# Attention and MLP on one core: softmax sums and weighted values in four 32-column tiles of the PE array, 112-token key tiles, one load per pair and tensor

## The chip, the core and the metric

The kernel runs on one core of a Trainium2 chip. The core's engines run side by side, each through a program of its own in order, and wait for one another through semaphores: TensorE (PE; PEld is its loading of the stationary operand), VectorE (DVE), ScalarE (ACT), GpSimd (POOL) and SyncE (SP, which here only issues DMAs). Sixteen DMA engines move data between HBM and the on-chip memory. The metric is the time of one execution in microseconds (us), the median of the runs. [...]

## What is computed

The sizes are B = 8 batches, H = 12 heads, S = 448 tokens and D = 64 per head; the MLP is 768 to 2048 to 768.

```
scores = scale * np.matmul(q, k.transpose(0, 1, 3, 2))
m = np.max(scores, axis=-1, keepdims=True)
e = np.exp(scores - m)
attn = e / (np.sum(e, axis=-1, keepdims=True) + np.exp(-m) + 1e-09)
attn_out = np.matmul(attn, v)

x = attn_out.transpose(0, 2, 1, 3).reshape(B * S, H * D)
h = x @ w_in
sp = np.where(h > 20.0, h, np.log1p(np.exp(np.minimum(h, 20.0))))
out = (h * np.tanh(sp)) @ w_out
```

With the maximum cancelled, a weight is exp(s) / (1 + sum of exp(s)). The kernel computes it so: no maximum is taken, and the reciprocal is exp(-ln(1 + sum)).

## The kernel before

The unit of attention is a **pair** j: two heads of one batch, 48 pairs in all, six to a batch. The program goes slot by slot. Slot j holds the scores of pair j, the weighted values of pair j-1, the loads of pair j+4 and the casts of pair j+2, and between them pieces of MLP work, called units: `mm1` is one block of 128 hidden columns of the batch before (six matmuls of 448 columns), `mm2` half of one block of the output of the batch before that (eight matmuls of 384 columns). Batch p = 0 (slots 0 to 5) has no units, batch p = 1 (slots 6 to 11) only mm1 units, later batches both. The order on every engine is the order of this text, since the schedule is manual.

Scores are computed transposed: keys on the partitions, queries along the columns. The 448 keys of a head are three tiles of 128 and a tail of 64. Each full tile of the two heads is two matmuls (L165), each of 64 rows, one in the upper and one in the lower half of the array. The tails of both heads stand in one 128-row block-diagonal tile `k_tail` and take one matmul (L177). ACT writes the exponentials `e` (L172 for full tiles, L178 for the tail).

`attend` multiplies `e` with `v_aug`, whose 128 columns are the 64 values of one head beside 64 columns of ones, so that one result `av` holds the weighted values in one half of its partitions and the sum of the weights, repeated, in the other half. It takes six matmuls of 128 rows (L188) and two of 64 rows for the tails (L197). ACT makes ln(1 + sum) of each head (L205) and exp(-ln) of both (L206), and `normalize` multiplies on DVE, one head at a time (L216), into `xT`, the transposed input of the MLP.

Loads of a pair are seven DMAs on SP: the first 384 tokens of q, k and v for both heads (L79: qm, km, vm), the tails of q and k (L91) and two tails of v (L86). POOL casts to bfloat16 (L104, L107, L113, L114). For pairs of batch 0 PE transposes q and k (L141, L146) and DVE copies the result; for the others two DMA transposes on SP do it (L121 for the full tiles, L125 for the tails), after which POOL copies the tail of k into `k_tail` (L137).

PSUM has three pools of two buffers: `s_ps` for scores (two banks each), `x_ps` for `av` and PE transposes, `m_ps` for mm1 and mm2 results. After the last mm1 unit of a batch (slot i = 4 of the next) `mish` runs on ACT over all of `h_sb` (L249, L250) between two loads of ACT's function table; mm2 reads its result `gm`. While it runs PE has eight mm2 units of the older batch, in p = 1 none. The weights are loaded by POOL's queue, `w_in` in slots 1 to 4 and `w_out` in slots 6 to 9. Slot 48 attends the last pair, and the MLP of the last batch ends the program.

Of the kernel before, what the change touches and what calls it, by code (L numbers as in the profile page):

```python
# [8 lines left out]
FP32 = mybir.dt.float32  # L9
# [6 lines left out]
def kernel(  # L16
# [11 lines left out]

    nc = tc.nc
# [36 lines left out]
    for i in range(2):
        kt = singles.tile([128, 128], BF16, name=f"k_tail{i}")
        nc.vector.memset(kt, 0.0)
        k_tail.append(kt)

    loaded, cast, qk_t, e_t, av_t, x_t = {}, {}, {}, {}, {}, {}
    gm_t, gt_t = {}, {}

    def load(j):
        b, h0 = j // NPAIR, 2 * (j % NPAIR)
        tiles = {}
        for name, src in (("q", q), ("k", k), ("v", v)):
            main = stage.tile([128, 2, NT, D], FP32, tag=f"{name}m", name=f"{name}m")
            nc.sync.dma_start(  # L79
                out=main,  # L80
                in_=src[b, h0 : h0 + 2, 0:MAIN, :].rearrange("h (p t) d -> p h t d", t=NT),
            )
            if name == "v":
                tail = stage.tile([128, D], FP32, tag="vt", name="vt")
                for h in range(2):
                    nc.sync.dma_start(  # L86
                        out=tail[h * 64 : h * 64 + 64, :], in_=src[b, h0 + h, MAIN:S, :]
                    )
            else:
                tail = stage.tile([64, 2, D], FP32, tag=f"{name}t", name=f"{name}t")  # L90
                nc.sync.dma_start(  # L91
                    out=tail, in_=src[b, h0 : h0 + 2, MAIN:S, :].rearrange("h p d -> p h d")
                )
            tiles[name] = (main, tail)
        loaded[j] = tiles

    def do_cast(j):

        tiles = loaded.pop(j)
        mb = half.tile([128, 2 * NT, 2, D], BF16, tag="mb", name="mb")  # L100
        tb = half.tile([64, 2, 2, D], BF16, tag="tb", name="tb")
        for i, name in enumerate(("k", "q")):
            main, tail = tiles[name]
            nc.gpsimd.tensor_copy(  # L104
                out=mb[:, i * NT : (i + 1) * NT].rearrange("p t h d -> p h t d"), in_=main
            )
            nc.gpsimd.tensor_copy(out=tb[:, 1 - i], in_=tail)  # L107
        main, tail = tiles["v"]
        va = v_aug[j % NV]
        vr = va[:, 0 : 2 * NT, :].rearrange("p (t h) c -> p t h c", h=2)  # L110
        for h in range(2):
            c = h * D
            nc.gpsimd.tensor_copy(out=vr[:, :, h, c : c + D], in_=main[:, h, :, :])  # L113
            nc.gpsimd.tensor_copy(  # L114
                out=va[h * 64 : h * 64 + 64, 2 * NT, c : c + D],
                in_=tail[h * 64 : h * 64 + 64, :],
            )
        cast[j] = (mb, tb)
        if j >= NPAIR:
            qk = qk_pool.tile([128, 2 * S], BF16, tag="qk", name="qk")  # L120
            nc.sync.dma_start_transpose(  # L121
                out=qk[:, 0 : 2 * MAIN].rearrange("p (t c) -> p t c", c=128),
                in_=mb.rearrange("p t h d -> p (t h d)"),
            )
            nc.sync.dma_start_transpose(  # L125
                out=qk[:, 2 * MAIN : 2 * S].rearrange("p (t c) -> p t c", c=TAIL),
                in_=tb.rearrange("p t h d -> p (t h d)"),
            )
            qk_t[j] = qk

    def transposes(j):
        mb, tb = cast.pop(j)
        kt = k_tail[j % 2]
        if j >= NPAIR:
            for h in range(2):
                r = slice(h * 64, h * 64 + 64)
                nc.gpsimd.tensor_copy(out=kt[r, r], in_=qk_t[j][r, S + MAIN : 2 * S])  # L137
            return
        ps = x_pool.tile([128, 1024], BF16, tag="x", name="tr_ps")
        for t in range(2 * NT):  # L140
            nc.tensor.transpose(  # L141
                ps[:, t * 128 : (t + 1) * 128], mb[:, t].rearrange("p h d -> p (h d)"), ident
            )
# [269 lines left out]
```

## Time and profile before

| | us |
|---|---|
| median of 3 runs | 492.85 |
| lowest and highest | 492.05, 496.56 |
| the profiled execution | 497.37 |
| its span, first to last instruction | 495.6 |
| PE busy in the span | 441.5 |
| ACT busy | 297.9 |
| DVE busy | 169.6 |
| POOL busy | 144.6 |

The profiled execution is 4.5 us above the median of the runs. Its time is its span and 1.8 us around it. Busy time of PE contains the time in which a matmul passes through the array behind the next one, so what one matmul costs is read from the distance between starts. [...]

### The profile page before, as it was taken

The page shows a single profiled execution, that of the slowest core. Times are in us where ns is not written, and L with a number is a line of the kernel's source. Part 1 is how long each engine was busy: PE and PEld are TensorE (multiplying, and loading weights), DVE is VectorE, ACT ScalarE, POOL GpSimd, SP SyncE. Part 2 cuts the span into 40 slices and gives each one's busy share as a digit, 9 for nine tenths or more (in the row PEclk, how much of TensorE's full clock was granted, in tenths as well). Part 3 has the DMA queues.
Part 4 walks back from the last instruction along what each step waited for, and adds up shares of the span by engine and source line. Part 5 has one row for each costly group of instructions (what it writes and reads, how often), then busy time and mean ns, then how long its engine had stood idle before and what let it go on. Part 6 is the DMA issues. An engine that isn't in the chain of part 4 may idle for free.

```text
span 495.6 us, 7105 instructions
## 1 busy us (share of the span) xinstructions
PE 441.5 (89%) x2432; PEld 209.9 (42%) x2432; DVE 169.6 (34%) x288; ACT 297.9 (60%) x419; POOL 144.6 (29%) x482
## 2 busy tenths in 40 slices
PE   3677595828999899999998999999998999999995
PEld 1222142304445344554444444554453445555563
DVE  4222242402463155322651354325532444220121
ACT  3556553595669667765678675856776757643200
POOL 4544253423333144313342243232431430000000
PEclk9956697977999999999999999999999999999999
DMA  5699999951543464446453564365544620120112
GB/s 132 157 219 238 163 211 158 199 131 20 159 113 90 119 164 117 117 134 170 119 132 103 129 160 118 92 165 148 131 110 121 162 57 1 63 65 1 60 69 64
DMA packets 110373, 60.46 MB, mean 122 GB/s; under 512 B 64768, under 2 KB 106752, under 8 KB 110336
## 3 DMA queue, kind: packets, MB, share of 16 engines
q1 hardware_dynamic: 105088, 53.71, 42.8%
q0 software_dynamic: 5248, 6.29, 8.2%
q8 instruction: 19, 0.31, 0.3%
q14 instruction: 18, 0.15, 0.1%
HBM read 45.61 MB, written 11.01 MB: 114 GB/s over the span
## 4 chain that ended last, share of the span: by engine, by line
PE 80%; DMA 7%; ACT 6%; SPq 3%; POOL 1%; issue 1%; DVE 0%; POOLq 0%
PE o_ps L264 30%; PE h_ps L221 29%; PE av_ps L188 10%; PE s_ps L165 6%; DMA qk<-tb 3%; PE av_ps L197 3%; PE s_ps L177 2%; DMA vm<-in_v_dram 2%; ACT e L172 1%; ACT ln L205 1%; ACT gm L249 1%; DMA km<-in_k_dram 1%; DMA vt<-in_v_dram 1%; SPq L79 1%; ACT rc L206 1%
## 5 line engine op out<-in xcount | busy, mean ns | idle before, releaser
L221 PE MATMUL h_ps<-xT,w_in_sb 128*128 128x448 bf16 x768 | 158.6, 356 | 1.4 <-DVE xT L216 1.4
L172 ACT ACTIVATE e<-s_ps 128x896 bf16<-128x896 f32 x144 | 126.0, 909 | 32.8 <-PE s_ps L165 30.5
L264 PE MATMUL o_ps<-w_out_sb,gm 128*128 128x384 bf16 x768 | 132.0, 330 | 0.0
L205 ACT ACTIVATE ln<-av_ps 64x448 f32<-64x448 f32 x96 | 51.7, 539 | 117.8 <-PE av_ps L197 116.6
L229 DVE COPY h_sb<-h_ps 128x448 f32<-128x448 f32 x112 | 70.0, 625 | 108.2 <-PE h_ps L221 107.4
L221 PEld LDWEIGHTS <-w_in_sb 128*128 128x128 bf16 x768 | 73.4, 99 | 72.3 <-issue 11.2
L264 PEld LDWEIGHTS <-gm 128*128 128x128 bf16 x768 | 75.4, 99 | 52.7 <-issue 4.3
L216 DVE TENSOR_TENSOR xT<-av_ps,rc 64x448 bf16<-64x448 f32 x96 | 59.7, 622 | 81.4 <-ACT rc L206 79.5
L165 PE MATMUL s_ps<-qk 64*128 64x448 bf16 x288 | 52.4, 384 | 37.0 <-ACT e L172 26.6
L272 DVE COPY o_sb<-o_ps 128x384 f32<-128x384 f32 x56 | 31.2, 558 | 116.9 <-PE o_ps L264 116.3
L137 POOL COPY k_tail_97<-qk 64x64 bf16<-64x64 bf16 x42 | 9.8, 234 | 112.9 <-DMA qk<-tb 72.3
L165 PEld LDWEIGHTS <-qk 64*128 64x128 bf16 x288 | 14.2, 96 | 61.2 <-issue 49.6
L249 ACT ACTIVATE gm<-h_sb 128x1536 bf16<-128x1536 f32 x28 | 39.2, 1471 | 0.1
L137 POOL COPY k_tail_95<-qk 64x64 bf16<-64x64 bf16 x42 | 9.8, 234 | 76.3 <-DMA qk<-tb 48.2
L104 POOL CAST mb<-km 128x384 bf16<-128x384 f32 x48 | 24.2, 503 | 19.8 <-DMA km<-in_k_dram 17.2
L206 ACT ACTIVATE rc<-ln 128x448 f32<-128x448 f32 x48 | 27.7, 576 | 1.5
L178 ACT ACTIVATE e<-s_ps 128x448 bf16<-128x448 f32 x48 | 25.7, 536 | 0.0
L104 POOL CAST mb<-qm 128x384 bf16<-128x384 f32 x48 | 24.2, 503 | 0.0
L264 PE MATMUL o_ps<-w_out_sb,gt 128*128 128x384 bf16 x128 | 22.0, 326 | 0.0
L233 ACT ACTIVATE gm<-h_ps 128x384 bf16<-128x384 f32 x16 | 7.9, 491 | 19.2 <-PE h_ps L221 19.2
L188 PE MATMUL av_ps<-e,v_aug_89 128*128 128x448 bf16 x72 | 18.0, 389 | 0.5 <-DVE k_tail_97 L153 0.5
L188 PE MATMUL av_ps<-e,v_aug_87 128*128 128x448 bf16 x72 | 18.0, 389 | 0.5 <-DVE k_tail_95 L153 0.5
(56 smaller groups left out, 262.7 us busy)
## 6 DMA issues: line engine op xcount, KB each, us to landing
qm<-in_q_dram SPq DMA_DIRECT2D x48, 192.0 KB, 2.8
km<-in_k_dram SPq DMA_DIRECT2D x48, 192.0 KB, 2.8
vm<-in_v_dram SPq DMA_DIRECT2D x48, 192.0 KB, 2.8
out_dram<-o_sb SPq DMA_DIRECT2D x24, 384.0 KB, 2.7
w_in_sb<-in_moe_w_in_dram POOLq DMA_DIRECT2D x4, 768.0 KB, 9.0
w_out_sb<-in_moe_w_out_dram POOLq DMA_DIRECT2D x4, 768.0 KB, 7.7
qt<-in_q_dram SPq DMA_DIRECT2D x48, 32.0 KB, 2.7
kt<-in_k_dram SPq DMA_DIRECT2D x48, 32.0 KB, 2.8
```

What stands on the lines that cost most here:

```text
L104: nc.gpsimd.tensor_copy(out=mb[:, i * NT : (i + 1) * NT].rearrange("p t h d -> p h t d"), in_=main)
L165: nc.tensor.matmul(sp[:, h, 0:S], lhsT=qk[r, t * 128 : (t + 1) * 128], rhs=qk[r, MAIN : MAIN + S], start=True, stop=True,)
L172: nc.scalar.activation(out=e[:, 2 * t : 2 * t + 2, :], in_=sp[:, :, 0:S], func=AF.Exp, scale=SCALE)
L188: nc.tensor.matmul(av[h][:, 0:S], lhsT=va[:, 2 * t + h, :], rhs=e[:, 2 * t + h, :], start=(t == 0), stop=False,)
L205: nc.scalar.activation(out=ln[r, :], in_=av[h][o, 0:S], func=AF.Ln, bias=1.0)
L206: nc.scalar.activation(out=rc, in_=ln, func=AF.Exp, scale=-1.0)
L216: nc.vector.tensor_mul(x_t[b][r, hp, :], av[h][r, 0:S], rc[r, :])
L221: nc.tensor.matmul(hp[:, 0:S], lhsT=w_in_sb[:, dm, ff * 128 : (ff + 1) * 128], rhs=x_t[b][:, dm, :], start=(dm == 0), stop=(dm == DM_T - 1),)
L229: nc.vector.tensor_copy(out=h_sb[:, ff, :], in_=hp[:, 0:S])
L249: nc.scalar.activation(out=gm[:, f, :], in_=h_sb[:, f, 0:MAIN], func=AF.Mish)
L264: nc.tensor.matmul(op[:, 0:HALF], lhsT=lhs, rhs=w_out_sb[:, ff, n * HALF : (n + 1) * HALF], start=(ff == 0), stop=(ff == FF_T - 1),)
L272: nc.vector.tensor_copy(out=o_sb[:, n * HALF : (n + 1) * HALF], in_=op[:, 0:HALF])
```

## The change

Attention goes by **groups** g of two pairs (four heads, three groups to a batch). The 448 keys are four tiles of 112 (token 4p + t on partition p of tile t), so there is no tail, no `k_tail` and no `v_aug`. Scores take eight matmuls per pair, two per tile, and four exponentials of 112 x 896. `sums(g)` adds up the weights of four heads: for each key tile four matmuls whose stationary operand is 112 x 32 ones and whose results go to partitions 0, 32, 64 and 96 on; ACT makes the reciprocal `rc` of all four heads with one Ln and one Exp. `attend(g, s)` does the same with 32 of the 64 value columns (every second one, s = 0 or 1), and one DVE multiplication writes `xT`. Both stand in even slots only, for the two pairs before. The rows of `w_in` are loaded in the order that fits. `den` and the PE transposes take buffers of `m_ps`.

Loads of a pair are three DMAs, in the order k, q, v, of 1,024 bytes per partition and head; they are issued after the casts and the DMA transpose of their slot, no longer ahead of them, and their staging has three buffers instead of four. One DMA transpose does q and k. DVE casts q and k of the pairs of batch 0, POOL the rest. `w_in` is loaded in slots 0 to 3 and `w_out` in slots 5 to 8. A block of 128 output rows is stored by two DMAs instead of one.

```diff
-    NT = S // 128
+    NT = 4
+    P = S // NT
-    stage = ctx.enter_context(tc.tile_pool(name="stage", bufs=4))
+    stage = ctx.enter_context(tc.tile_pool(name="stage", bufs=AHEAD - 1))
+    v_pool = ctx.enter_context(tc.tile_pool(name="v", bufs=6))
+    e_pool = ctx.enter_context(tc.tile_pool(name="e", bufs=3))
...
+        for name in names:
+            src = {"q": q, "k": k, "v": v}[name]
+            st = stage.tile([P, 2, NT * D], FP32, tag=name, name=f"{name}_f")
             nc.sync.dma_start(
+                out=st, in_=src[b, h0 : h0 + 2].rearrange("h (p t) d -> p h (t d)", t=NT)
+            )
...
+            nc.sync.dma_start_transpose(
+                out=qk.rearrange("c i (t p) -> c (i t) p", p=P),
+                in_=mb.rearrange("p i t h d -> p (i t h d)"),
+            )
...
+        ps = m_pool.tile([128, 2, S], BF16, tag="m", name="tr_ps")
...
+        for t in (2 * part, 2 * part + 1):
             sp = s_pool.tile([128, 2, 512], FP32, tag="s", name="s_ps")
             for h in range(2):
                 r = slice(h * D, h * D + D)
                 nc.tensor.matmul(
+                    sp[0:P, h, 0:S],
+                    lhsT=qk[r, 0, t * P : (t + 1) * P],
+                    rhs=qk[r, 1, :],
...
+    def side_by_side(ps, g, weights):
         for t in range(NT):
+            for c in range(4):
                 nc.tensor.matmul(
+                    ps[c * 32 : c * 32 + 32, 0:S],
+                    lhsT=weights(2 * g + c // 2, c % 2, t),
+                    rhs=e_t[2 * g + c // 2][:, t, c % 2, :],
                     start=(t == 0),
+                    stop=(t == NT - 1),
                 )
+    def sums(g):
+        den = m_pool.tile([128, 512], FP32, tag="m", name="den_ps")
+        side_by_side(den, g, lambda j, h, t: ones[0:P, :])
         rc = work.tile([128, S], FP32, tag="rc", name="rc")
+        nc.scalar.activation(out=rc, in_=den[:, 0:S], func=AF.Ln, bias=1.0)
+        nc.scalar.activation(out=rc, in_=rc, func=AF.Exp, scale=-1.0)
+        rc_t[g] = rc
+    def attend(g, s):
...
+        av = x_pool.tile([128, 512], FP32, tag="x", name="av_ps")
+        side_by_side(
+            av, g, lambda j, h, t: v_t[j][:, h, t, :].rearrange("p (d s) -> p s d", s=2)[:, s, :]
+        )
+        nc.vector.tensor_mul(x_t[b][:, gi, s, :], av[:, 0:S], rc_t[g])
...
-            if j + 4 < J:
-                load(j + 4)
+            g = j // 2 - 1 if j % 2 == 0 and j >= 2 else None
             if j + 2 < J:
-                do_cast(j + 2)
-            if 1 <= j <= 4:
-                load_w_in(j - 1)
-            if 6 <= j <= 9:
-                load_w_out(j - 6)
+                do_cast(j + 2, nc.vector if j + 2 < NPAIR else nc.gpsimd)
+                cast_v(j + 2)
+            if j + AHEAD < J:
+                load(j + AHEAD)
+            if j <= 3:
+                load_w_in(j)
+            if 5 <= j <= 8:
+                load_w_out(j - 5)
             rest = max(0, len(units) - 2)
             if j < J:
                 scores(j, 0)
             take(1)
             if j + 1 < J:
                 transposes(j + 1)
+            if g is not None:
+                sums(g)
             take(1)
-            if j >= 1:
-                attend(j - 1)
             if j < J:
                 scores(j, 1)
             take((rest + 1) // 2)
-            if j >= 1:
-                normalize(j - 1)
+            if g is not None:
+                attend(g, 0)
+                attend(g, 1)
             take(len(units), last=True)
```

On PE, before, the end of the weighted values of one pair (two results, av0 and av1, one per head) and the second half of the next pair's scores, then an mm1 unit:

```order
L188 LDWEIGHTS v_aug0_87
L188 MATMUL av1_ps_2047<-e_1926,v_aug0_87 128x448
L197 LDWEIGHTS v_aug0_87
L197 MATMUL av0_ps_2046<-e_1926,v_aug0_87 128x448
L197 LDWEIGHTS v_aug0_87
L197 MATMUL av1_ps_2047<-e_1926,v_aug0_87 128x448
L165 LDWEIGHTS qk_1829
L165 MATMUL s_ps_2061<-qk_1829 128x448
```

On PE, with the change, the end of an mm1 unit in an even slot and the first of four key tiles of a group's weighted values (`e` and `v_b` of its two pairs):

```order
L179 MATMUL h_ps_2475<-xT_1842,w_in_sb_88 128x448
L146 LDWEIGHTS v_b_1954
L146 MATMUL av_ps_2484<-e_2235,v_b_1954 32x448
L146 LDWEIGHTS v_b_1954
L146 MATMUL av_ps_2484<-e_2235,v_b_1954 32x448
L146 LDWEIGHTS v_b_2158
L146 MATMUL av_ps_2484<-e_2360,v_b_2158 32x448
L146 LDWEIGHTS v_b_2158
L146 MATMUL av_ps_2484<-e_2360,v_b_2158 32x448
```

Eight matmuls per pair with 128 result partitions became 24 with 32, of which four stand together, and they moved out of every slot into every second one.

On SP, before, one slot of a later batch, from two stores to the DMA transposes:

```order
L276 DMA out_dram<-o_sb 128x768 x2
L79 DMA qm<-in_q_dram 128x2x192
L91 DMA qt<-in_q_dram 64x2x64
L79 DMA km<-in_k_dram 128x2x192
L91 DMA kt<-in_k_dram 64x2x64
L79 DMA vm<-in_v_dram 128x2x192
L86 DMA vt<-in_v_dram 64x64 x2
L121 DMA_TRANSPOSE qk<-mb 128x6x128
L125 DMA_TRANSPOSE qk<-tb 128x2x64
```

On SP, with the change, such a slot:

```order
L219 DMA out_dram<-o_sb 112x768
L219 DMA out_dram<-o_sb 16x768
L92 DMA_TRANSPOSE qk<-mb 128x8x112
L77 DMA k_f<-in_k_dram 112x2x256
L77 DMA q_f<-in_q_dram 112x2x256
L77 DMA v_f<-in_v_dram 112x2x256
```

Nine issues for a pair became four, and the transpose moved ahead of the loads.

On ACT, before, around the `mish` of batch 1:

```order
L178 ACTIVATE e<-s_ps 128x448
L249 ACT_TABLE_LOAD
L249 ACTIVATE gm<-h_sb 128x1536 x4
L250 ACTIVATE gt<-h_sb 128x16x64
L251 ACT_TABLE_LOAD
L172 ACTIVATE e<-s_ps 128x896 x2
L205 ACTIVATE ln<-av_ps 64x448 x2
L206 ACTIVATE rc<-ln 128x448
L172 ACTIVATE e<-s_ps 128x896
```

On ACT, with the change, the same place:

```order
L159 ACTIVATE rc<-rc 128x448
L136 ACTIVATE e<-s_ps 112x896 x2
L207 ACT_TABLE_LOAD
L207 ACTIVATE gm<-h_sb 128x1536 x4
L208 ACTIVATE gt<-h_sb 128x16x64
L209 ACT_TABLE_LOAD
L136 ACTIVATE e<-s_ps 112x896 x6
L158 ACTIVATE rc<-den_ps 128x448
```

Behind `mish` six exponentials now stand in a row, where two Ln and an Exp stood after the first two.

## Rows read from the trace of the kernel before

**Rows 1.** Busy time by stretch: busy us (x count) by engine, PEclk, DMA share, GB/s.

```profile
8.60:53.60 45.00, 29.70 (x124) 9.40 (x122) 10.60 (x25) 26.17 (x40) 21.12 (x62) 0.70 0.96 198
53.60:113.40 59.80, 39.59 (x188) 15.77 (x186) 17.47 (x28) 36.82 (x50) 24.60 (x78) 0.84 0.88 170
113.40:438.40 325.00, 318.35 (x1811) 154.47 (x1810) 128.77 (x211) 221.00 (x294) 95.72 (x328) 0.99 0.45 115
```

**Rows 2.** Timeline of PE, 148 to 178 us: start, length, what [idle before].

```profile
147.73 1.30 PE L188 MATMUL av_ps<-e,v_aug_93 128*128 128x448 bf16 x6
148.96 0.36 PE L197 MATMUL av_ps<-e,v_aug_93 64*128 64x448 bf16 x2
149.16 0.35 PE L165 MATMUL s_ps<-qk 64*128 64x448 bf16 x2
149.44 0.36 PE L177 MATMUL s_ps<-qk,k_tail_95 128*128 128x448 bf16 x1
149.64 2.43 PE L221 MATMUL h_ps<-xT,w_in_sb 128*128 128x448 bf16 x12
151.91 10.56 PE L264 MATMUL o_ps<-w_out_sb,gm 128*128 128x384 bf16 x64
162.41 0.55 PE L165 MATMUL s_ps<-qk 64*128 64x448 bf16 x4
...
167.13 0.80 PE L165 MATMUL s_ps<-qk 64*128 64x448 bf16 x4 [2.15 <-ACT e L172]
```

**Rows 3.** Timeline of all engines, 200.6 to 201.0 us.

```profile
200.69 0.10 PEld L197 LDWEIGHTS <-v_aug_89 64*128 64x128 bf16 x2 [0.37 <-issue]
200.69 0.36 PE L197 MATMUL av_ps<-e,v_aug_89 64*128 64x448 bf16 x2
200.70 0.10 PEld L165 LDWEIGHTS <-qk 64*128 64x128 bf16 x2
200.89 0.35 PE L165 MATMUL s_ps<-qk 64*128 64x448 bf16 x2
```

**Rows 4.** Timeline of PE, 28 to 40 us.

```profile
29.52 0.99 PE L165 MATMUL s_ps<-qk 64*128 64x448 bf16 x4 [1.74 <-ACT e L172]
...
37.62 0.99 PE L165 MATMUL s_ps<-qk 64*128 64x448 bf16 x4 [1.74 <-ACT e L172]
```

**Rows 5.** Timeline of ACT, 28 to 40 us.

```profile
35.05 1.10 ACT L205 ACTIVATE ln<-av_ps 64x448 f32<-64x448 f32 x2 [3.21 <-PE av_ps L197]
```

**Rows 6.** Timeline of SP's DMA issues, 46 to 84 us.

```profile
50.23 0.57 SPq L79 DMA_DIRECT2D qm<-in_q_dram  x1
...
54.81 1.25 SPq L121 DMA_TRANSPOSE qk<-mb  x1
...
57.38 0.58 SPq L79 DMA_DIRECT2D qm<-in_q_dram  x1
```

**Rows 7.** Timeline of PE, 50 to 114 us.

```profile
81.81 0.93 PE L165 MATMUL s_ps<-qk 64*128 64x448 bf16 x4 [5.22 <-DMA qk<-tb]
...
109.45 0.56 PE L165 MATMUL s_ps<-qk 64*128 64x448 bf16 x2 [8.19 <-ACT e L172]
...
113.72 0.50 PE L264 MATMUL o_ps<-w_out_sb,gm 128*128 128x384 bf16 x1
```

**Rows 8.** Costliest groups of the page: busy us, mean ns of one | idle before.

```profile
L172 ACT ACTIVATE e<-s_ps 128x896 bf16<-128x896 f32 x144 | 126.0, 909 | 32.8 <-PE s_ps L165 30.5
L205 ACT ACTIVATE ln<-av_ps 64x448 f32<-64x448 f32 x96 | 51.7, 539 | 117.8 <-PE av_ps L197 116.6
L272 DVE COPY o_sb<-o_ps 128x384 f32<-128x384 f32 x56 | 31.2, 558 | 116.9 <-PE o_ps L264 116.3
L178 ACT ACTIVATE e<-s_ps 128x448 bf16<-128x448 f32 x48 | 25.7, 536 | 0.0
```

**Rows 9.** DMA issues of the page: KB each, median us from issue to landing.

```profile
qm<-in_q_dram SPq DMA_DIRECT2D x48, 192.0 KB, 2.8
qt<-in_q_dram SPq DMA_DIRECT2D x48, 32.0 KB, 2.7
```

More of the change, by code (lines that the diff above doesn't have):

```diff
@@ L66, with load @@
[L66 to L74, printed above, removed]
+    loaded, cast, qk_t, v_t, e_t, x_t = {}, {}, {}, {}, {}, {}
+    rc_t, gm_t, gt_t = {}, {}, {}
+    def load(j, names="kqv"):
         b, h0 = j // NPAIR, 2 * (j % NPAIR)
-        tiles = {}
-        for name, src in (("q", q), ("k", k), ("v", v)):
-            main = stage.tile([128, 2, NT, D], FP32, tag=f"{name}m", name=f"{name}m")
+        for name in names:
+            src = {"q": q, "k": k, "v": v}[name]
+            st = stage.tile([P, 2, NT * D], FP32, tag=name, name=f"{name}_f")
@@ L128, in do_cast, with cast_v @@
             )
             qk_t[j] = qk
+        else:
+            cast[j] = mb
+    def cast_v(j):
+        vb = v_pool.tile([P, 2, NT, D], BF16, tag="v", name="v_b")
+        nc.gpsimd.tensor_copy(out=vb.rearrange("p h t d -> p h (t d)"), in_=loaded.pop((j, "v")))
+        v_t[j] = vb
     def transposes(j):
-        mb, tb = cast.pop(j)
-        kt = k_tail[j % 2]
         if j >= NPAIR:
-            for h in range(2):
-                r = slice(h * 64, h * 64 + 64)
-                nc.gpsimd.tensor_copy(out=kt[r, r], in_=qk_t[j][r, S + MAIN : 2 * S])
@@ L138, in transposes @@
             return
[L139 to L143, printed above, removed]
-        for t in range(2):
-            c = 2 * MAIN + t * TAIL
-            nc.tensor.transpose(
-                ps[:, c : c + TAIL], tb[:, t].rearrange("p h d -> p (h d)"), ident[0:64, 0:64]
-            )
-        qk = qk_pool.tile([128, 2 * S], BF16, tag="qk", name="qk")
@@ L154, in transposes @@
+        qk = qk_pool.tile([128, 2, S], BF16, tag="qk", name="qk")
+        nc.vector.tensor_copy(out=qk, in_=ps)
         qk_t[j] = qk
     def scores(j, part):
-        qk, kt = qk_t[j], k_tail[j % 2]
+        qk = qk_t[j]
         if part == 0:
-            e_t[j] = work.tile([128, 2 * NT + 1, S], BF16, tag="e", name="e")
-        e = e_t[j]
-        for t in (0, 1) if part == 0 else (2,):
+            e_t[j] = e_pool.tile([P, NT, 2, S], BF16, tag="e", name="e")
+        for t in (2 * part, 2 * part + 1):
@@ new lines, in attend @@
+    def attend(g, s):
+        b, gi = divmod(g, GRP)
+        if gi == 0 and s == 0:
+            x_t[b] = work.tile([128, GRP, 2, S], BF16, tag="xT", name="xT")
+        av = x_pool.tile([128, 512], FP32, tag="x", name="av_ps")
[3 more added lines that the diff above has]
+        nc.vector.tensor_mul(x_t[b][:, gi, s, :], av[:, 0:S], rc_t[g])
+        if s == 1:
+            for j in (2 * g, 2 * g + 1):
+                e_t.pop(j), v_t.pop(j)
+            rc_t.pop(g)
```

162 lines of the change are left out of this document (51 added, 111 removed).

## The prediction

> **What bounds the kernel now.** I read the busy time by stretch first, since an average over this program hides three stages [rows 1]. From 113.4 to 438.4 us (batches 2 to 7) PE is busy 318.35 of 325.00 us at PEclk 0.99, ACT 221.00, DVE 128.77, the DMA engines 45%: PE sets the time, and every 0.1 us of PE per pair counts 36 times. From 8.6 to 53.6 us (batch 0, six slots without MLP units) PE is busy 29.70 of 45.00 us at PEclk 0.70, ACT 26.17, and the DMA engines 96%: nobody is full but the DMAs. From 53.6 to 113.4 us (batch 1) PE has 39.59 of 59.80 us, the DMAs 88%.
>
> The timelines say what the two early stages wait for. In batch 0 PE and ACT wait for each other: from one slot's scores to the next (29.52 to 37.62) 8.10 us pass, PE waits 1.74 us for the exponentials [rows 4], and ACT's Ln waits 3.21 us for the weighted values [rows 5]. SP is nearly full there: from the first load of one pair to that of the next (50.23 to 57.38) 7.15 us, and the seven loads and two transposes stand back to back [rows 6]. In batch 1 PE waits 5.22 us for a DMA transpose at 81.81, and 8.19 us behind `mish` at 109.45; mm2 starts at 113.72 [rows 7]. Behind `mish` of batches 2, 4 and 6 there is a wait of 2.15 us, since slot i = 5 has no units there [rows 2].
>
> **PE, what one pair costs.** Starts in steady state give the prices [rows 2]. A 448-column matmul steps by 2.27 / 12 = 0.189 us (149.64 to 151.91). The six full matmuls of `attend` take 1.23 us to the first tail matmul (147.73 to 148.96), which is 5 x 0.189 and a last step of 0.285: going from 128 rows to 64 costs 0.10 us. Two 64-row matmuls in the two halves of the array start in the same 0.01 us, and the next two 0.20 us behind (200.69, 200.89) [rows 3]: they run side by side at 0.20 us per two. Back to 128 rows the step is 0.28 us (149.16 to 149.44), so that way costs 0.08 [rows 2]. A pair before is: first half of the scores 0.10 + 0.20 + 0.28 = 0.58, `attend` 1.43 (147.73 to 149.16), second half 0.48 (149.16 to 149.64). Sum 2.49 us.
>
> After: both halves of the scores are two steps of 64 rows, 2 x 0.58 = 1.16. A group has three times four key tiles, 12 steps of four column tiles. No row shows column tiles. The lower bound of a step is 0.189 us (all four at once, as one matmul), the upper 4 x 0.189 = 0.76 (one after another). I take 0.20, from the nearest row, the two row tiles of rows 3: these are independent parts of one array too, with their own operands. Mode changes into and out of `sums` and of the two `attend` together are four at 0.09. A group: 12 x 0.20 + 0.36 = 2.76, a pair 1.38. Sum 2.54 us, or +0.05 per pair. So four tiles side by side save one matmul step in seven, and more mode changes and a fourth score tile take it back: **PE gains nothing even where the tiles work perfectly.**
>
> [...]
>
> Two smaller costs. Stationary operands of 112 columns and of 32 appear in no row; a load of 128 columns takes 0.10 us, and across a mode change it cannot run ahead [rows 3]. Extra exposure is at least 0 and at most such a load at each of two entries to scores per pair, 0.2; I take 0.05 per pair, near zero, because within a mode the load of the next scores starts 0.01 us behind the running matmul. With 0.05 from above, 38 pairs of steady PE: **+3.8 us** (0 to +9). Second, `den` takes a buffer of `m_ps` between the two halves of an open mm2 block, so in slots i = 0 of batches 2 to 7 the next block gets the buffer that was just finished and waits for its copy: 0.558 us of DVE [rows 8] and some 0.35 for the matmul to leave the array (its record is 0.36 long [rows 3]), less 0.58 of scores in between: 0.33 each, **+2 us** (0 to +3).
>
> **ACT, DVE, POOL.** ACT per pair before: 3 x 0.909 + 0.536, two Ln of 0.539 and one Exp of about that, 4.9 us; after, 4 x 0.909 and half of two 128 x 448 operations, 4.2 us [rows 8]. From 113.4 us on that and the halved DVE multiplications lie under PE and bring nothing. Behind `mish` in slots without units, four exponentials in place of three and a half with Ln and Exp between: PE's wait stays about 2 us there, `mish` itself the same.
>
> **The early stages.** Here the change takes away what is waited for. SP issues four DMAs per pair instead of nine: by rows 6 some 0.6 us a load and 1.25 a transpose, 7.15 becomes 3.1 us. The block `k_tail`, its copies on POOL and the second transpose go. In batch 0 the loop through PE, Ln and Exp is run once per two pairs. The floor of a slot is ACT's work, 4.2 us; PE at the lower clock, with transposes, needs about 5 in an even slot plus its share of waiting. I take 5.0 per slot for 7.5 before (45.0 / 6): -15 us for six. DMA speaks against a full gain: at 0.96 busy it moved 198 GB/s [rows 1], of which a pair is 3 x (192 + 32) KB [rows 9], 3.5 us at all engines or 7 at half of them while `w_in` runs. So the gain of batch 0 lies between -21 (floor of ACT) and -3 (7 us a slot).
>
> Batch 1 then starts earlier and meets the same weights. Up to 113.4 us the DMA engines worked about 4 + 43.2 + 52.6 = 100 us (the last two are share times length [rows 1], the first an allowance for the 8.6 us ahead of them). If all of it had to land before mm2 starts, that could not come before some 98 us; but loads up to four pairs ahead are in it and need not, 4 x 3.5 = 14 us. So mm2's start, 113.7 before, lies between 84 and 110. The 5.22 us wait for the transpose should shrink, since the transpose no longer stands behind the loads. I take the earlier start of the first cast (three issues ahead of all three tensors of the pair, not seven) as 1.5 us in it, and 96 for mm2's start: **-18 us** (-4 to -29).
>
> **Sum.** -18 + 3.8 + 2 = -12 us. The profiled execution took 497.37, so it would be about 485; the median of the runs is 4.5 lower, and the forecast for it is 492.85 - 12 = **481 us** (own range 469 to 497: -29 + 5 and -4 + 8).
>
> **Rivals.** (1) The column tiles don't run four at once. Each step is then P instead of 0.20 us, on 19 groups of 12 steps behind 113 us: 228 x (P - 0.20). The change is slower than before from P = 0.25 on. Two at a time (P about 0.39) gives 481 + 43 = 524; one at a time (0.76) 609. For it: four different moving operands of 112 rows, which no row here shows; the two of rows 3 come from different rows. Against: issue is no limit, since two loads and two matmuls start within 0.01 us there. Chance 0.10. (2) The stationary loads of a step wait until the array is free, as at a mode change: P = 0.28, +18, **499 us**, slower. [...] The trace disagrees for row halves: at 200.70 loads for both halves start while both compute [rows 3]. Chance 0.08. (3) The early gain doesn't come, because the weights fill the DMA engines whoever asks first: -4 + 6, **495 us**, within 1% of before. For it 0.96 and 0.88 DMA share [rows 1]; against it the waits of rows 4 and 5, in which no DMA stands. Chance 0.15.
>
> **How the numbers follow.** Forecast 0.67, rivals 0.10, 0.08, 0.15. The predicted time is the forecast's. The range leaves out rival 1 and the best tail of the forecast: 469 to 503. About 1% (487.9 to 497.8 us) is what a measurement of this kernel can tell from no change. Faster than that: most of the forecast, 0.60, and a third of rival 3, 0.05; slower: rivals 1 and 2, 0.18; the rest, 0.17, is the same.
>
> **What would show it.** In the new profile: steps of four 32-column matmuls starting within about 0.02 us and 0.20 us apart (right), or staggered (rival 1), or with 0.28 us between (rival 2); the first mm2 at about 96 us; slots of batch 0 of about 5 us; from there to the end 5 to 6 us more than 382 (495.6 - 113.7). The prediction is wrong if batch 0 still takes 7 us per slot with DMA share near 1, or if the steady stage differs by more than 10 us in either direction.

## The result and the profile after

| | before | after |
|---|---|---|
| median | 493.36 (4 runs) | 480.2 (4 runs) |
| lowest and highest | 492.05, 496.56 | 478.21, 490.59 |
| the profiled execution | 497.37 | 478.21 |
| its span | 495.6 | 476.4 |
| first mm1 | 57.31 | 43.33 |
| first mm2 | 113.72 | 93.44 |
| from there to the end | 381.9 | 383.0 |

The ratio is 0.971, 95% interval 0.9633 to 0.9788: faster by 2.9%. The ratios here and below leave out executions more than 1.5% above the fastest of their kernel, here the one at 490.59; medians are of all. The two profiled executions lie 19.2 us apart, more than the medians (13.2), since that of before lies 4 us above its median and that of after 2 us below. In these two profiles all of the difference stands ahead of the first mm2 (20.3 us); behind it 1.1 us are lost. A second profile of the changed kernel (the last experiment) has the first mm2 at 91.66 and loses 4.1 us behind it. So the medians leave some 14 to 17 us for the early stages, an estimate from 13.2 + 1.1 and 13.2 + 4.1.

Rows by stretch of after (us, PE, PEld, DVE, ACT, POOL busy, PEclk, DMA share, GB/s; PEclk is the clock granted to TensorE as a share of its full speed), to be read against [rows 1]; the first ends shortly after the first mm1, the second shortly after the first mm2, the third ahead of the last MLP:

```profile
7.00:45.00 38.00, 28.54 (x247) 11.85 (x246) 11.90 (x22) 26.34 (x34) 16.30 (x24) 0.87 1.18 230
45.00:97.00 52.00, 35.92 (x249) 14.35 (x250) 12.17 (x20) 30.13 (x33) 15.52 (x25) 0.81 0.98 194
97.00:420.00 323.00, 316.84 (x2452) 149.23 (x2444) 106.58 (x176) 199.11 (x223) 57.46 (x94) 1.00 0.49 116
```

The last stretch is as full of PE as before: 316.84 of 323.00 us. PE's timeline of after in the early stages answers to [rows 4, 7]:

```profile
30.50 0.59 PE L129 MATMUL s_ps<-qk 64*112 64x448 bf16 x4
...
36.76 0.99 PE L129 MATMUL s_ps<-qk 64*112 64x448 bf16 x4 [3.64 <-DMA qk<-mb]
...
43.33 2.44 PE L179 MATMUL h_ps<-xT,w_in_sb 128*128 128x448 bf16 x12
51.71 0.99 PE L129 MATMUL s_ps<-qk 64*112 64x448 bf16 x4 [5.94 <-DMA qk<-mb]
52.64 4.54 PE L179 MATMUL h_ps<-xT,w_in_sb 128*128 128x448 bf16 x12
...
90.45 0.62 PE L129 MATMUL s_ps<-qk 64*112 64x448 bf16 x2 [9.57 <-ACT e L136]
...
93.44 2.74 PE L231 MATMUL o_ps<-w_out_sb,gm 128*128 128x384 bf16 x8
```

L129 is the score matmul, L179 mm1, L231 mm2, L136 the exponentials. Slots 0 to 5 begin at 6.01 and slot 6 at 36.76: 5.1 us a slot, in it the 3.64 us for which slot 6 waits for the first DMA transpose of batch 1. Slot 7 waits 5.94 us for the second. These two are all that PE waits for DMA, 9.6 us, no less than the waits of that kind before (three, 9.4 us, the longest the 5.22 of [rows 7]). They cost more than themselves: behind the second the twelve matmuls of mm1 take 4.54 us where those at 43.33 take 2.44, since TensorE's clock had fallen while PE waited (PEclk 0.50 from 52.2 to 56.0 us). Where the waits come from stands in the timeline of SP's issues, to be read against [rows 6]:

```profile
23.98 1.34 SPq L92 DMA_TRANSPOSE qk<-mb  x1
...
29.66 7.45 SPq L92 DMA_TRANSPOSE qk<-mb  x1
37.15 0.94 SPq L77 DMA_DIRECT2D k_f<-in_k_dram  x1
...
42.29 9.87 SPq L92 DMA_TRANSPOSE qk<-mb  x1
52.20 0.74 SPq L77 DMA_DIRECT2D k_f<-in_k_dram  x1
```

A transpose (L92) that SP issues in 1.34 us at 23.98 holds SP for 7.45 and 9.87 us in the next two slots, and the loads of the slot stand behind it. POOL issues the first two quarters of `w_out` at 31.57 and 43.09, while these two are being issued. The DMA share doesn't tell the stretches of the three apart (1.18 from 23.98 to 29.66 us, 1.23 from 29.66 to 37.15, 1.19 from 42.29 to 52.20), but what the engines move does: 243, 199 and 139 GB/s. In the steady state, PE's timeline of after, against [rows 2]:

```profile
144.51 0.40 PE L129 MATMUL s_ps<-qk 64*112 64x448 bf16 x2 [0.82 <-ACT e L136]
145.32 0.40 PE L129 MATMUL s_ps<-qk 64*112 64x448 bf16 x2 [0.41 <-ACT e L136]
...
147.27 1.47 PE L231 MATMUL o_ps<-w_out_sb,gm 128*128 128x384 bf16 x8
148.67 0.94 PE L146 MATMUL den_ps<-e,ones 112*32 112x448 bf16 x16
149.54 1.47 PE L231 MATMUL o_ps<-w_out_sb,gm 128*128 128x384 bf16 x8
150.95 0.58 PE L129 MATMUL s_ps<-qk 64*112 64x448 bf16 x4
151.47 1.47 PE L231 MATMUL o_ps<-w_out_sb,gm 128*128 128x384 bf16 x8
152.87 1.70 PE L146 MATMUL av_ps<-e,v_b 112*32 112x448 bf16 x32
154.50 1.48 PE L231 MATMUL o_ps<-w_out_sb,gm 128*128 128x384 bf16 x8
```

Sixteen matmuls of `sums` take 0.94 us: three steps of 0.19 and a last matmul of 0.36. So four column tiles do the work of four matmuls in the time of one. The next two numbers are distances between starts. From the start of a group's first column tile to what follows is 0.87 and 1.63 us, and the steps into and out of column mode cost 0.09 and 0.10 (0.254 and 0.285 between starts instead of 0.163 and 0.189). A pair's share is half of 0.87 and 1.63 and one entry of 0.09, 1.34 us.

Within the column mode the loads of a step don't wait here until the array is free: those of the next four tiles start within 0.003 us of matmuls that take the same 112 rows (the matmul at 203.430 us and the load at 203.432, for one), and the step is 0.19 us, not the 0.28 of rival 2.

### The profile page after: what moved, and what is told of

It is laid out like the page before. It is cut to its first block, busy times and chain, and to the rows that moved or that the text cites. A ratio compares the mean times of both kernels' runs of the same rounds, so it can differ in the third digit from the quotient of the medians.

```text
span 476.4 us, 7816 instructions
## 1 busy us (share of the span) xinstructions
PE 434.7 (91%) x3248; PEld 205.3 (43%) x3248; DVE 140.6 (30%) x235; ACT 266.9 (56%) x323; POOL 90.6 (19%) x150
## 4 chain that ended last, share of the span: by engine, by line
PE 83%; DMA 10%; ACT 5%; SPq 1%; issue 0%; DVE 0%
PE h_ps L179 32%; PE o_ps L231 32%; PE s_ps L129 8%; PE av_ps L146 7%; DMA qk<-mb 5%; PE den_ps L146 4%; ACT e L136 3%; DMA v_f<-in_v_dram 3%; DMA k_f<-in_k_dram 1%; DMA q_f<-in_q_dram 1%; ACT gm L207 1%; SPq L77 1%; ACT L209 0%; ACT L207 0%; ACT gt L208 0%
## 5 line engine op out<-in xcount | busy, mean ns | idle before, releaser
L136 ACT ACTIVATE e<-s_ps 112x896 bf16<-112x896 f32 x192 | 164.2, 916 | 137.2 <-PE s_ps L129 137.1
L179 PE MATMUL h_ps<-xT,w_in_sb 128*128 128x448 bf16 x768 | 163.3, 357 | 0.0
L231 PE MATMUL o_ps<-w_out_sb,gm 128*128 128x384 bf16 x768 | 133.3, 328 | 0.0
L179 PEld LDWEIGHTS <-w_in_sb 128*128 128x128 bf16 x768 | 68.9, 98 | 85.5 <-issue 31.9
L231 PEld LDWEIGHTS <-gm 128*128 128x128 bf16 x768 | 73.4, 98 | 57.0 <-issue 10.3
L129 PE MATMUL s_ps<-qk 64*112 64x448 bf16 x384 | 64.0, 398 | 31.5 <-ACT e L136 19.5
L86 POOL CAST mb<-k_f 112x512 bf16<-112x512 f32 x42 | 25.9, 617 | 184.3 <-DMA k_f<-in_k_dram 159.7
L129 PEld LDWEIGHTS <-qk 64*112 64x112 bf16 x384 | 20.2, 131 | 70.1 <-issue 55.8
L102 POOL CAST v_b<-v_f 112x512 bf16<-112x512 f32 x48 | 29.6, 616 | 88.0 <-PE av_ps L146 62.6
L146 PE MATMUL av_ps<-e,v_b 112*32 112x448 bf16 x768 | 42.9, 367 | 0.0
L170 DVE TENSOR_TENSOR xT<-av_ps,rc 128x448 bf16<-128x448 f32 x48 | 30.0, 625 | 40.3 <-PE av_ps L146 38.3
L86 POOL CAST mb<-q_f 112x512 bf16<-112x512 f32 x42 | 25.9, 616 | 13.6 <-DMA q_f<-in_q_dram 13.0
L146 PEld LDWEIGHTS <-v_b 112*32 112x32 bf16 x768 | 18.9, 99 | 22.3 <-issue 9.1
L146 PE MATMUL den_ps<-e,ones 112*32 112x448 bf16 x384 | 25.3, 388 | 0.0
L231 PE MATMUL o_ps<-w_out_sb,gt 128*128 128x384 bf16 x128 | 22.0, 326 | 0.0
L231 PEld LDWEIGHTS <-gt 128*128 128x128 bf16 x128 | 12.0, 98 | 9.5 <-issue 2.0
```

The source lines that it names most:

```text
L86: eng.tensor_copy(out=mb[:, i].rearrange("p t h d -> p h t d"), in_=loaded.pop((j, name)).rearrange("p h (t d) -> p h t d", d=D),)
L102: nc.gpsimd.tensor_copy(out=vb.rearrange("p h t d -> p h (t d)"), in_=loaded.pop((j, "v")))
L129: nc.tensor.matmul(sp[0:P, h, 0:S], lhsT=qk[r, 0, t * P : (t + 1) * P], rhs=qk[r, 1, :], start=True, stop=True,)
L136: nc.scalar.activation(out=e_t[j][:, t], in_=sp[0:P, :, 0:S], func=AF.Exp, scale=SCALE)
L146: nc.tensor.matmul(ps[c * 32 : c * 32 + 32, 0:S], lhsT=weights(2 * g + c // 2, c % 2, t), rhs=e_t[2 * g + c // 2][:, t, c % 2, :], start=( ...
L170: nc.vector.tensor_mul(x_t[b][:, gi, s, :], av[:, 0:S], rc_t[g])
```

## Experiments

Lines are those of the changed kernel unless a heading says otherwise. No kernel leaves out work. A run's ratio is to the kernel before on the same chip, whose medians were 493.87 (the runs up to "the old loop"), 496.07 (up to "loads first") and 493.56 (the rest).

**Program order of the column tiles** (a single execution).

```diff
-        for t in range(NT):
-            for c in range(4):
+        for c in range(4):
+            for t in range(NT):
```

> The changed kernel with the two loops of the column tiles exchanged: all four key tiles of one column tile, then the next column tile. Same matmuls, same number. Theory (the tiles gain only because four different ones stand next to each other): matmuls of one tile follow at 0.189 us, so 16 of them take about 2.5 to 3.0 us instead of 0.76, a group 5 to 7 us more, and the kernel 570 to 615 us. Rival (the engine finds the free tile by itself, or the price of 16 matmuls is one of their number): no change, 478 to 482 us.

Measured 494.52, outside both forecasts. My theory had 570 us or more. PE's timeline of this kernel:

```profile
217.17 0.97 PE L146 MATMUL den_ps<-e,ones 112*32 112x448 bf16 x16
...
221.40 1.73 PE L146 MATMUL av_ps<-e,v_b 112*32 112x448 bf16 x32
```

0.97 and 1.73 us stand against 0.94 and 1.70. In the program four matmuls of one tile now stand ahead of the next tile's first; one tile after the other would take some 3 us (16 x 0.189). The trace doesn't name the tile of a matmul, but its starts come in four waves 0.19 us apart, with four starts 0.013 us apart in each, which fits four tiles that each go through their own four matmuls. The theory that tiles share a step only where neighbours in the program are in different tiles is false.

The column tiles don't explain the longer time. It lies mostly ahead of mm2, which starts at 107.13 for 93.44: five waits for `qk<-mb` with 19.9 us. Since the changed kernel itself had executions at 490.59 and 493.03, one execution can't say whether this kernel is slower. The waits are the theme of the next runs.

**Many issues again**: one load per head and tensor, and two DMA transposes.

```diff
-            nc.sync.dma_start(
-                out=st, in_=src[b, h0 : h0 + 2].rearrange("h (p t) d -> p h (t d)", t=NT)
+            for h in range(2):
+                nc.sync.dma_start(
+                    out=st[:, h, :], in_=src[b, h0 + h].rearrange("(p t) d -> p (t d)", t=NT)
...
-            nc.sync.dma_start_transpose(
+            for i in range(2):
+                nc.sync.dma_start_transpose(
```

> The changed kernel with each load cut in two (one DMA per head) and the DMA transpose cut in two (k, q): eight issues on SP per pair instead of four, same bytes, same packets. Theory (the early gain comes from the loop through PE and ACT in batch 0, run once per two pairs): SP then needs about 6 x 0.6 + 2 x 1.25 = 6.1 us per pair, only a little above the slots of batch 0 (5.1 us), which start ahead; 481 to 484 us. Rival (the issues on SP set the slots of batch 0, 7.15 us per pair before): slots of batch 0 go to 6 us or more and the first mm2 from 93 to 99 us or later; 486 to 492 us.

482.67 (479.72 to 484.37), ratio 0.978 (0.9723 to 0.9837). Eight DMAs per pair instead of four cost 2.5 us by the medians, and the intervals overlap. The first mm2 starts at 93.98 (93.44), so the early stages are as they were, and the fewer issues, which the prediction named first, bring little. From mm2 to the end this execution takes 388.6 us (383.0). That is mostly TensorE's clock: PE's timeline of this kernel behind `mish`, to be read against 1.47 and 0.94 us at 147.27 and 148.67 of after:

```profile
148.29 2.74 PE L233 MATMUL o_ps<-w_out_sb,gm 128*128 128x384 bf16 x8
150.96 1.69 PE L148 MATMUL den_ps<-e,ones 112*32 112x448 bf16 x16
```

PEclk is 0.91 from 140 to 180 us and 0.96 from 220 to 260 and from 340 to 380, where it is 1.00 in after. PE had waited for exponentials behind `mish` just before, as it does in after, whose clock stayed up. The unchanged kernel shows the same fall in its second profile (last experiment), so it can't be put down to the issues.

**Weights one slot later**, as in the kernel before: `w_in` in slots 1 to 4, `w_out` in 6 to 9.

```diff
-            if j <= 3:
-                load_w_in(j)
-            if 5 <= j <= 8:
-                load_w_out(j - 5)
+            if 1 <= j <= 4:
+                load_w_in(j - 1)
+            if 6 <= j <= 9:
+                load_w_out(j - 6)
```

> The changed kernel with both weights loaded where the kernel before loads them, w_in in slots 1 to 4, w_out in 6 to 9, one slot later. Theory (what is left to wait for in slots 6 and 7, 3.6 and 5.9 us for a DMA transpose, is due to weights that hold the DMA engines): some 3 to 6 us of the waits go, 474 to 477 us. Rival (the engines have the same sum of work to do before mm2, the order does not matter): 478 to 482 us.

489.2 (482.72 to 491.69), ratio 0.9875 (0.9786 to 0.9965), 9 us above after by the medians. The interval just touches that of after, and lies above that of its second measurement (0.964 to 0.9744); mm2 starts at 102.92. My theory was wrong by its sign. Rows by stretch, after and then this kernel:

```profile
60.00:80.00 20.00, 20.00 (x177) 8.48 (x180) 8.39 (x14) 12.28 (x16) 7.10 (x12) 1.00 1.17 245
```

```profile
60.00:80.00 20.00, 10.83 (x82) 4.50 (x80) 5.62 (x9) 5.49 (x7) 3.83 (x6) 0.88 1.23 126
```

The DMA engines are as busy (1.23 against 1.17), but move half as much, 126 for 245 GB/s, and PE works 10.83 of 20 us. The DMA issues of 40 to 100 us (KB each, median us to landing), after and this kernel:

```profile
w_out_sb<-in_moe_w_out_dram POOLq DMA_DIRECT2D x3, 768.0 KB, 11.3
...
qk<-mb SPq DMA_TRANSPOSE x7, 6.1
```

```profile
w_out_sb<-in_moe_w_out_dram POOLq DMA_DIRECT2D x4, 768.0 KB, 19.5
...
qk<-mb SPq DMA_TRANSPOSE x6, 17.6
```

A transpose lands after 17.6 us instead of 6.1. Averaged over the trace's packets, one 256-byte packet of a transpose takes 0.026 us from 60 to 80 us of after, 0.027 in the steady state of both kernels, and 0.080 (60 to 80 us) and 0.102 (80 to 100 us) in this kernel. PE's waits (us in total, times, longest), after and then this kernel:

```profile
PE s_ps L129 <- ACT e L136: 19.5, 24, 9.6
PE s_ps L129 <- DMA qk<-mb: 9.6, 2, 5.9
```

```profile
PE s_ps L129 <- DMA qk<-mb: 23.9, 6, 10.3
```

**The old loop, attend moved** (the kernel before): in batch 0 `attend(j-1)` behind the second half of the scores of j, so that PE has scores to do while ACT makes the exponentials.

```diff
-            if j >= 1:
+            if j >= NPAIR:
                 attend(j - 1)
...
                 scores(j, 1)
+            if 1 <= j < NPAIR:
+                attend(j - 1)
```

> The kernel before, and in batch 0 alone the weighted values of pair j-1 behind the second half of the scores of pair j, so that ACT makes all exponentials of a slot before Ln and Exp. Theory (the loop PE to ACT to PE sets the slots of batch 0): slots of batch 0 fall from 7.5 to about 6 us, some of it is lost again to DMA waits in batch 1, 484 to 489 us. Rival (SP's issues or the DMA engines set these slots): slots stay, 492 to 495 us.

496.37 (490.77 to 499.32, 10 runs), ratio 1.0037 (0.9989 to 1.0084). Slot 5 begins at 38.62 instead of 45.71, so the loop does get 7 us shorter; slot 6 begins where it did, 52.66 for 52.98. PE's timeline of this kernel says on what:

```profile
52.66 0.93 PE L165 MATMUL s_ps<-qk 64*128 64x448 bf16 x4 [7.47 <-DMA qk<-tb]
```

The shorter loop runs into the DMA transposes of batch 1. This suggests two limits, one behind the other; the run with both lifted, below, tests it.

**No DMA transposes in batch 1**: PE transposes q and k of pairs 6 to 11 as it does those of batch 0.

```diff
-        if j >= NPAIR:
+        if j >= 2 * NPAIR:
             qk = qk_pool.tile([128, 2, S], BF16, tag="qk", name="qk")
...
     def transposes(j):
-        if j >= NPAIR:
+        if j >= 2 * NPAIR:
             return
```

> The changed kernel with the q and k of batch 1 transposed by PE as those of batch 0, so no DMA transpose runs while weights are loaded. Theory (what ends last in batch 1 is the DMA transpose that shares the engines with w_out; its waits on PE were 9.6 us in the profile of the changed kernel and 19.9 and 23.9 in those of e1 and e3): the waits go, PE pays some 0.7 us for each of six pairs, 469 to 475 us, and the executions lie within 4 us. Rival (the engines have too much to load in any case, and the wait moves to the loads): 478 to 484 us.

468.63 (468.33 to 471.46), ratio 0.9483 (0.9421 to 0.9545): 11.6 us below after. Slot 6 begins at 32.33, the first mm1 at 38.49, mm2 at 83.41, and from there to the end it is 383.0 as after. PE's waits of this kernel:

```profile
PE s_ps L129 <- ACT e L136: 19.9, 26, 9.6
```

The line for `qk<-mb` is gone, and the rest is as after but for four short waits of 1.2 us in all. In the profiles the gain ahead of mm2 is 10.0 us. The waits account for 9.6 of them; so what PE now pays for the transposes of six pairs must be nearly what a higher clock gives back. Rows by stretch, after and then this kernel (PEclk 0.75 and 1.00):

```profile
40.00:60.00 20.00, 14.06 (x78) 5.40 (x77) 4.37 (x7) 5.63 (x7) 5.42 (x9) 0.75 1.17 195
```

```profile
40.00:60.00 20.00, 19.04 (x155) 8.95 (x154) 9.55 (x16) 9.74 (x12) 6.46 (x12) 1.00 1.15 241
```

**The same in the kernel before** (in `do_cast` and `transposes` there).

```diff
-        if j >= NPAIR:
+        if j >= 2 * NPAIR:
             qk = qk_pool.tile([128, 2 * S], BF16, tag="qk", name="qk")
...
-        if j >= NPAIR:
+        if j >= 2 * NPAIR:
             for h in range(2):
```

> The kernel before with the same single edit, q and k of batch 1 transposed by PE. Theory (the supply of transposed q and k ends last there too): 481 to 487 us, most of what the whole change gave. Rival (SP's seven load issues per pair bound the early stages, and they stay): 489 to 495 us.

493.1 (492.29 to 493.68, 10 runs), ratio 0.9968 (0.9929 to 1.0006); mm2 at 109.43. A better supply alone changes nothing there. My theory of a gain of 6 us or more fell; that the loop through PE, Ln and Exp is what limits is tested below.

**After's loads and 112-token tiles, but before's attend per pair**: `v_aug` of 128 columns, Ln twice, Exp and two multiplications per pair, in every slot, and the rows of `w_in` in their old order.

```diff
-        side_by_side(
-            av, g, lambda j, h, t: v_t[j][:, h, t, :].rearrange("p (d s) -> p s d", s=2)[:, s, :]
-        )
-        nc.vector.tensor_mul(x_t[b][:, gi, s, :], av[:, 0:S], rc_t[g])
+        for t in range(NT):
+            for h in range(2):
+                nc.tensor.matmul(
+                    av[h][:, 0:S],
+                    lhsT=va[:, 2 * t + h, :],
+                    rhs=e[:, t, h, :],
```

> The loads, the 112-token key tiles, the casts, the single DMA transpose and the order of loads of the changed kernel, with the weighted values of the kernel before: per pair and slot, v beside ones in 128 columns, eight full-width matmuls, two Ln, one Exp, two multiplications; no column tiles, no groups. Theory (the gain comes with the loads and the layout, the column tiles give nothing): PE 2.67 us per pair for 2.57, so 4 us above the changed kernel, 482 to 487 us. Rival (the groups, with Ln and Exp once per two pairs and PE freed in odd slots, carry the gain): 490 to 496 us.

503.92 (502.35 to 512.09), ratio 1.0173 (1.01 to 1.0247): slower than both. PE's timeline of this kernel in the steady state:

```profile
243.99 1.68 PE L157 MATMUL av_ps<-e,v_aug 112*128 112x448 bf16 x8
245.60 0.58 PE L139 MATMUL s_ps<-qk 64*112 64x448 bf16 x4
```

Eight matmuls of full width take 1.61 us to the next start where the kernel before took 1.43, and the column tiles of after 1.34 per pair. With the score halves a pair is 0.61 + 1.61 + 0.52 = 2.74 us, 0.17 more than after, or 6.5 us in 38 pairs. From mm2 to the end this kernel takes 393.8 us, 11 more than after; part of the rest is TensorE's clock (PEclk 0.99 from 120 to 420 us, 1.00 in after), and 18 of 62 halves of the scores that take 0.72 us instead of 0.52. mm2 starts at 106.7, 13 us later; slots of batch 0 take 6.5 us instead of 5.1, which is 8 of them. My theory, 482 to 487 us, fell, and the loss went beyond the rival's 490 to 496. So new tiles and new loads alone lose; groups in column tiles are what makes the layout pay, on PE and in the loop. This run takes away groups and column tiles together, so it doesn't say which of them brings the shorter slots.

**Loads first**: loads ahead of casts and transposes as in the kernel before, with a fourth staging buffer.

```diff
+            if j + AHEAD < J:
+                load(j + AHEAD)
             if j + 2 < J:
...
-            if j + AHEAD < J:
-                load(j + AHEAD)
```

> The changed kernel with the loads of pair j+4 ahead of the casts and the DMA transpose of pair j+2 on SP, and four staging buffers, as in the kernel before. Theory (the prediction's step: a transpose behind three loads comes later, and PE waits for it): waits for transposes grow by 3 to 8 us, 483 to 488 us. Rival (the engines share their time between all that is under way, whoever was issued first): 478 to 482 us.

484.47 (482.56 to 490.86), ratio 0.9778 (0.9706 to 0.985); mm2 at 99.15, waits for `qk<-mb` of 16.7 us in place of 9.6. The new order on SP is worth some 4 us by the medians, but the intervals overlap, and the edit adds a buffer beside the order.

**Both limits lifted in the kernel before**: the edits of the two runs on it together.

```diff
-        if j >= NPAIR:
+        if j >= 2 * NPAIR:
...
-            if j >= 1:
+            if j >= NPAIR:
                 attend(j - 1)
...
+            if 1 <= j < NPAIR:
+                attend(j - 1)
```

> The kernel before with the edits of e4 and e6 together: in batch 0 the weighted values behind the second half of the scores, and the q and k of batch 1 transposed by PE. Alone neither moved the time by 1%. Theory (batch 0 has two limits one behind the other, the loop through PE and ACT and the supply of transposed q and k; lifting one shows the other): both lifted give 8 us or more, 480 to 487 us. Rival (SP's seven load issues per pair are a third limit of the same height): 489 to 494 us.

486.8 (486.37 to 486.96), ratio 0.9863 (0.9802 to 0.9923). Each edit by itself moved nothing that can be told apart from no change; together they give 6.8 us, and mm2 starts at 102.76. PE's timeline shows what is late next:

```profile
28.54 0.50 PE L141 MATMUL tr_ps<-ident,mb 128*128 128x128 bf16 x6 [1.85 <-DVE xT L216]
```

Before's PE transposes take a buffer of `x_ps`, and so wait for `normalize` of the pair before; slots take 6.64 us. In after they use `m_ps`. With PE transposes the changed kernel starts mm2 at 83.41, so 19 us of its lead remain; no run says how they divide among groups, buffers and fewer loads.

**No stall behind `mish`**, on top of PE transposes: four of the mm2 units that ran during `mish` are kept for slot i = 5, which has none in batches 2, 4 and 6.

```diff
-                    first, m2 = m2[:8], m2[8:]
+                    first, m2 = m2[: max(0, len(m2) - 4)], m2[max(0, len(m2) - 4) :]
```

> The kernel of e5 with four mm2 units left for slot i = 5 in every batch from 2 on, instead of none in batches 2, 4 and 6: behind mish fewer units, in slot 5 four. Theory (PE waits 2.3 us three times because slot 5 has only exponentials): these waits go, 6 us less than e5, 461 to 464 us. Rival (PE then waits for mish itself, as mish ends only 3.6 us ahead of the units): 467 to 470 us.

461.46 (460.21 to 462.49, 6 runs), ratio 0.9346 (0.9305 to 0.9387), the fastest here, 6.5% below the kernel before. PE's timeline of this kernel has no wait where after had 2.05 us:

```profile
121.97 5.36 PE L231 MATMUL o_ps<-w_out_sb,gm 128*128 128x384 bf16 x32
127.26 0.59 PE L129 MATMUL s_ps<-qk 64*112 64x448 bf16 x4
127.78 2.77 PE L231 MATMUL o_ps<-w_out_sb,gm 128*128 128x384 bf16 x16
130.48 0.59 PE L129 MATMUL s_ps<-qk 64*112 64x448 bf16 x4
131.00 2.77 PE L231 MATMUL o_ps<-w_out_sb,gm 128*128 128x384 bf16 x16
```

Over the run with PE transposes alone the gain is 7.2 us by the medians; three such waits are 6.2.

**PE transposes and later weights together.**

```diff
-        if j >= NPAIR:
+        if j >= 2 * NPAIR:
...
-            if 5 <= j <= 8:
-                load_w_out(j - 5)
+            if 6 <= j <= 9:
+                load_w_out(j - 6)
```

> The kernel of e5 with the weights one slot later, the edit of e3. In e3 it cost 9 us. Theory (what e3 lost is that DMA transposes and w_out share the engines longer; without transposes in that stretch nothing is lost): 466 to 471 us. Rival (later weights are late for mm1 and mm2 themselves): 474 to 480 us.

468.0 (467.54 to 469.71), ratio 0.9489 (0.9438 to 0.954). The later weights, which cost 9 us beside DMA transposes, cost nothing without them. So it is the meeting of the two that costs, not the late `w_out`.

**After once more**, unchanged.

> The changed kernel as it is, once more and in more rounds, beside the runs above. Both theories: 478 to 485 us; by the theory that transposes and w_out collide by chance of their timing, the executions lie 8 us or more apart, those of e5 and e11 within 4.

478.85 (475.73 to 493.03, 6 runs), ratio 0.9692 (0.964 to 0.9744). Five executions lie within 5.2 us, less than the 8 that were expected, and one at 493.03; those of the five kernels with PE transposes in batch 1 lie 0.6 to 3.1 us apart. So the spread goes with the DMA transposes. That transposes and `w_out` collide by chance of their timing isn't shown, since the execution at 493.03 left no trace. In the profiled one mm2 starts at 91.66, and PE waits 9.4 us for `qk<-mb` in four waits. From mm2 to the end it is 386.0 us, 3 more than in the first profile: PEclk is 0.96 from 140 to 180 us and from 220 to 260, and the eight matmuls of mm2 behind `mish` (146.07) take 2.43 us instead of 1.47.

## Why the prediction was right, and where it was off

The forecast of 481 us holds, 480.2 measured, partly by luck, because two terms that were off nearly cancel: the early gain some 14 to 17 us by the medians instead of 18, the later loss 1.1 and 4.1 in two profiles instead of 5.8. TensorE's clock, which makes these two profiles differ, stands in none of the terms behind mm2.

- **"PE gains nothing even where the tiles work perfectly"**: right against the kernel before. Four tiles take steps of 0.19 (0.20 assumed), a mode change 0.09 to 0.10. A score half in 112-column mode takes 0.61, not 0.58, since the step after its mode change is 0.234 instead of 0.200; there the 112-column loads take 0.123 to 0.126 us, those of 128 columns 0.092 to 0.095. A pair is 2 x 0.614 + 1.34 = 2.57 us, 0.08 more than before, where 0.10 was assumed. The other side of that sentence was missing from the prediction: with 112-token tiles of full width a pair costs 0.17 us more, and the column tiles win that back.
- **"`den` takes a buffer of `m_ps`", +2 us**: it didn't occur. In the timeline above mm2 goes on at 151.47 without a wait, while DVE still copies the finished block, as DVE's timeline of after shows:

```profile
151.06 0.56 DVE L239 COPY o_sb<-o_ps 128x384 f32<-128x384 f32 x1 [7.28 <-PE o_ps L231]
```

  So the next block doesn't write the buffer that is being copied; the term took for granted that it would.
- **From mm2 to the end "5 to 6 us more"**: it was 1.1, and 4.1 in the second profile, 3 of them by the clock. In the first profile 4.7 us are missing. Two of them are that buffer wait, 0.8 the smaller PE term (0.02 in 38 pairs). The rest is mostly a wait of the kernel before that I had not seen, since as part of a run of four matmuls it has no bracket. PE's timeline of before, two first halves of the scores:

```profile
229.55 0.55 PE L165 MATMUL s_ps<-qk 64*128 64x448 bf16 x4
...
236.60 0.71 PE L165 MATMUL s_ps<-qk 64*128 64x448 bf16 x4
```

  The second is 0.16 longer. Its fourth load starts at 236.95, and ACT's exponential of the tail, which holds the score buffer, ends at 236.90. Of the 28 such halves from 123 to 358 us 15 are of this length, 2.4 us together. After has no tail and no such wait: its halves are 0.58 to 0.59.
- **ACT, DVE, POOL under PE bring nothing**: right. The wait behind `mish` "stays about 2 us": 0.82 + 3 x 0.41 = 2.05 for 2.15.
- **The early stages, -18**: 20.3 in the profiles and some 14 to 17 by the medians. A slot of batch 0 was taken as 5.0 and is 5.1. The mechanism named for it, that the loop PE, Ln, Exp runs once per two pairs, is borne out by the run with before's attend in after (6.5 us a slot). But the loop alone would have brought nothing: the run that shortened it in the kernel before hit the transposes. Lifting both there gave 6.8 us, so the gain comes of both and of more that no run takes apart.
- **SP's 7.15 us per pair become 3.1**: so it looks in quiet slots, but it isn't what is saved; eight DMAs for four move the first mm2 by 0.5 us.
- **"The 5.22 us wait for the transpose should shrink, since the transpose no longer stands behind the loads"**: this step failed. Two waits of 9.6 us in all remain. The order may help (4 us by the medians, loads first), but what the transpose waits for is mostly the DMA engines, where it shares them with the weights, and there the issue itself holds SP for up to 9.87 us.
- **Rivals 1 and 2** are out: steps of 0.19 us. **Rival 3**, that the weights fill the DMA engines whoever asks first, was wrong as a whole and right in one place: it is the transposes that suffer, and taking them off the DMA engines gave 11.6 us more.

What stays open: when TensorE's clock falls behind `mish` and when it doesn't, after the same waits; what lets a transpose run at full pace beside `w_out` in one execution (after, 60 to 80 us, 245 GB/s) and not in another (the same stretch with weights one slot later, 126 GB/s). Whether column tiles run past the program's order in other shapes wasn't tried.

## What to carry to other kernels

Where two resources limit a stage one behind the other (here a loop between engines and the supply of transposed operands), an edit that lifts one shows nothing; before an idea is dropped, its run should be read for what is late next. Transposes by DMA beside the load of the weights cost 11.6 us here: try to keep them out of such a stretch, and let PE do them there, if it waits anyway. A wait of PE can cost more than its length, since the clock may be down when it ends (behind the wait of 5.94 us twelve matmuls took 4.54 us for 2.44, at PEclk 0.50); so look at PEclk before a difference between two profiles is put down to an edit. Splitting narrow results over four column tiles costs PE no more than one matmul here (0.19 us for four), besides 0.09 to 0.10 us at each change of mode, and fills the array where a stationary operand would else carry columns of ones.

## What the hardware showed that I had not expected

- Four column tiles of the PE array don't need to alternate in the program: with all four key tiles of one column tile ahead of the next in the program, 16 matmuls took 0.97 us instead of 0.94, where one tile after the other would take some 3 (an estimate, 16 x 0.189).
- Loads for a column tile start within 0.003 us of matmuls that take the same 112 rows, and the step stays 0.19 us.
- Beside a weight load DMA transposes can run at two paces: in one profile 126 GB/s instead of 245 at about the same busy share, and a landing after 17.6 us instead of 6.1; the issue of one transpose held SP for 9.87 us and of another for 1.34.
- After the same waits behind `mish` PE went on at the full clock in one execution (eight matmuls of mm2 in 1.47 us, PEclk 1.00 from 140 to 180 us) and at a lower one in others (2.43 and 2.74 us, PEclk 0.96 and 0.91 there); after's first eight, at 93.44 us and PEclk 0.50, took 2.74.
